# Chunk 1's softmax tiles turned by DMA, half of a key load held behind them, and a new order list

## The chip, the cores and the metric

The kernel runs on one core of one Trainium2 chip. The metric is the device time of one execution in microseconds; of several executions the median is given. A second figure, the span, runs from the first to the last of the program's own instructions in the one execution that was profiled.

## What is computed

Sorted block attention, and behind it a feed-forward layer with a cosine gate. `sort_net` is made nearly doubly stochastic by five rounds of normalising; it mixes the eight key blocks and the eight value blocks of each head; each query block attends to its mixed block alone; the result goes through two matrices.

```python
P = sort_net                                     # (4, 8, 8, 8)
for _ in range(5):
    P = exp(P - max(P, -1)); P = P / (sum(P, -1) + 1e-9); P = P / (sum(P, -2) + 1e-9)
k_sorted = einsum('bhij,bhjcd->bhicd', P, k_b)   # blocks of 96 rows, 8 blocks, d = 64
v_sorted = einsum('bhij,bhjcd->bhicd', P, v_b)
scores = (q_b @ k_sorted^T) / 8                  # 96 x 96 for each block
attn = exp(scores - max); attn = attn / sum
x = (attn @ v_sorted), heads side by side        # (3072, 512)
h = x @ w_in                                     # 512 -> 2048
out = (h * cos(h)) @ w_out                       # 2048 -> 512
```

## The kernel before

The 3072 output rows are cut into eight chunks of 384 rows. Chunk n belongs to batch n // 2 and holds four query blocks u = 0..3 of that batch. Batches 0 and 1 are the first pair, 2 and 3 the second; a pair's keys and values are loaded and sorted together.

The program is one hand-written list, `PLAN`, of some 800 short lines. Each line calls one small function with its numbers, and the order of the lines is the order in which every engine gets its instructions. Nothing reorders them: each engine runs its own in order and waits where a semaphore says so. So the list decides which instruction stands behind which wait. The lines that matter here, for chunk n and block u:

- `S n u` is the score unit: eight matmuls with 128 rows, query block against sorted keys. `T n u` makes the same scores with eight matmuls of 64 rows; two neighbours of these take different halves of the array.
- `M` (VectorE, maximum of the scores), `X` (VectorE, subtract it), `E` (ScalarE, exp, into one of three tiles `p_buf`).
- The softmax tile must be turned before it meets the values. There are two ways. `TP` turns it with eight TensorE transposes into PSUM (tile `pps`) and `TE` copies it to `pT`. `TD` does both with one DMA transpose that SyncE issues.
- `AV` is the product of the turned tile and the sorted values, eight matmuls (tile `av`); `N` divides (VectorE); `XP` and `XE`, or `XD` by DMA, turn the result into `xT`.
- `U n f` (tile `h`, eight matmuls of 384 columns), `C` (ScalarE, the cosine), `G` (VectorE, the product) and `D n t q` (tile `o`, four matmuls of 512 columns: rows t, quarter q of the sum) are the two matrices. `U n f 1` and `U n f 2` run one or both of their halves as twice as many matmuls of 192 columns. `O` copies a finished 128-row block out of PSUM and `W` sends it to DRAM through SyncE.
- `ks`/`kse` sort the keys of batch 1, `vb`/`vbe` its values, `kg`/`kge` the keys of the second pair. `QP`/`QE` turn queries on TensorE.
- `Lpk z 2` loads half z of the second pair's keys into the tile `pair` (128 partitions, 768 KB written); `Lq` loads queries and `Lpv` values. These are issued by GpSimd. `vp2` has GpSimd reorder values from `kv` to `vperm` in four copies. `hp n u` is a tiny GpSimd copy of one column of `pT`: it makes GpSimd, and every load behind it, wait until that tile has been written.

PSUM has three two-bank tiles (`big`) and two one-bank tiles (`acc`). Warm-up matmuls (`keep_warm`) run while the first loads arrive; `MORE` says how many extra pieces they are cut into.

Of the kernel before, what the change touches and what calls it, by code (L numbers as in the profile page):

```python
# [13 lines left out]
ALU = mybir.AluOpType  # L14
AX = mybir.AxisListType

MORE = 55
PLAN = """\
vp 32
kp 0 B 1  # L20
# [116 lines left out]
QE 1 0 1 A  # L137
Lq 2
Lpk 0 2
Lpk 1 2  # L140
G4 1 0
D 0 0 1
vp2 64 128
S 1 2 B
S 1 0 B
M 1 2
S 1 3 B
D 0 1 0
M 1 0
D 0 1 1  # L150
X 1 2
D 0 1 2
X 1 0
E 1 2 1
ks 4 B
D 0 1 3
M 1 3
E 1 0 2
TP 1 2 B
D 0 0 2  # L160
# [60 lines left out]
Lq 3
hk
Lpv 0 6
Lpv 1 6
QE 2 1 0 V
Lpv 2 6
QD 3
zeros 4
C 1 0
G 1 0  # L230
vbe 1 A
vb 0 c
# [46 lines left out]
D 1 0 1
E 2 0 2  # L280
G 1 7
E 2 1 0
S 2 2 B
TD 2 0
D 1 0 2
kg 0 c
kge 0 A
M 2 2
X 2 2
E 2 2 1  # L290
TD 2 1
TD 2 2
S 2 3 B
M 2 3
D 1 0 3
O 1 0 o A
W 1 0
hp 2 2
Lpv 3 6
# [24 lines left out]
AV 2 1
N 2 1
TP 2 3 c
TE 2 3 A
D 1 2 0
AV 2 2
N 2 2  # L330
E 3 0 0
AV 2 3
XP 2 1 B
XE 2 1 V
N 2 3
W 1 1
XP 2 0 c
XE 2 0 V
D 1 2 1
D 1 2 2  # L340
kg 5 B
XP 2 3 B
XP 2 2 c
kge 5 A
XE 2 2 V
XE 2 3 V
D 1 2 3
O 1 2 o V
TD 3 0
W 1 2  # L350
U 2 0
C 2 0
G 2 0
kg 6 B
QD 4
# [36 lines left out]
U 2 6
S 3 2 c 1
M 3 2 1
U 2 7
C 2 6
G 2 6
C 2 7
G 2 7
T 3 3 B  # L400
E 3 1 1
TD 3 1
X 3 2 1
E 3 2 2
TD 3 2
M 3 3
X 3 3
D 2 0 0
D 2 0 1
E 3 3 0  # L410
vgT 0 8 B
TD 3 3
ones 1
AV 3 0
N 3 0
XD 3 0
D 2 0 2
D 2 0 3
O 2 0 o V
W 2 0  # L420
vge 0 8 A
D 2 1 0
vgT 2 8 B
T 4 0 B
AV 3 1
vge 2 8 A
hp 3 3
Lq 5
M 4 0
X 4 0  # L430
D 2 2 0
N 3 1
XD 3 1
D 2 1 1
D 2 1 2
D 2 1 3
O 2 1 o A
AV 3 2
N 3 2
# [64 lines left out]
C 3 6
G 3 6
vge 14 4 A
S 4 2 c 1
M 4 2 1
X 4 2 1
U 3 7  # L510
C 3 7
T 4 3 B
T 5 0 B
G 3 7
M 4 3
X 4 3
E 4 1 2
TD 4 1
E 4 2 0
TD 4 2  # L520
D 3 0 0
D 3 0 1
D 3 0 2
M 5 0
X 5 0
E 4 3 1
TD 4 3
AV 4 0
N 4 0
XD 4 0  # L530
D 3 0 3
D 3 1 0
O 3 0 v A
D 3 1 1
AV 4 1
N 4 1
S 5 1 B
M 5 1
X 5 1
E 5 1 0  # L540
E 5 0 2
XD 4 1
TD 5 0
TD 5 1
QD 6
D 3 1 2
D 3 1 3
AV 4 2
N 4 2
D 3 2 0  # L550
AV 4 3
N 4 3
O 3 1 v A
D 3 2 1
D 3 2 2
# [24 lines left out]
W 3 2  # L580
U 4 3
C 4 3
G 4 3
U 4 5
C 4 5
G 4 5
X 5 2 1
U 4 4
C 4 4
G 4 4  # L590
U 4 6
U 4 7
C 4 6
G 4 6
C 4 7
S 5 3 B
M 5 3
G 4 7
E 5 2 1
TD 5 2  # L600
D 4 0 0
AV 5 0
X 5 3
E 5 3 2
N 5 0
TD 5 3
XD 5 0
D 4 0 1
D 4 0 2
S 6 0 B  # L610
AV 5 1
D 4 1 0
# [15 lines left out]
O 4 0 v A
N 5 2
XD 5 2  # L630
O 4 1 v A
# [12 lines left out]
C 5 1
S 6 3 c 0
D 4 2 3
G 5 1
O 4 2 v V
U 5 0
C 5 0  # L650
G 5 0
U 5 2
C 5 2
U 5 3
QD 7
M 6 3 0
G 5 2
S 6 3 c 1
U 5 4
C 5 3  # L660
G 5 3
X 6 3 0
W 4 0
W 4 1
C 5 4
G 5 4
W 4 2
# [164 lines left out]
def kernel(  # L832
# [16 lines left out]
    B, H, S, D = q.shape  # L849
# [129 lines left out]
    vv = kv[:, :128 * D].rearrange("p (c d) -> p d c", d=D)  # L979
    VQ = 16  # L980

    def v_permute(rows, lo=0, halves=True):

        for z in range(lo, D, VQ):
            dst = vperm[rows, :CD].rearrange("p (d c) -> p d c", d=D)[:, z:z + VQ]
            src = vv[rows, z:z + VQ, :blk]
            if halves:
                dst = dst.rearrange("p d (x t) -> p d x t", x=2)  # L990
                src = src.rearrange("p d (t x) -> p d x t", x=2)
            nc.gpsimd.tensor_copy(dst, src)  # L992
# [72 lines left out]
    V, A = nc.vector, nc.scalar  # L1065
# [31 lines left out]
    E, Q = E_eps[:, :, :nb], Q_eps[:, :nb]  # L1097
# [502 lines left out]
    def spv():  # L1600
# [7 lines left out]
        vp=vp, vp2=vp2, z_vperm=z_vperm, p_pads=p_pads, pk2=pk2, bl2=bl2, sp2=sp2, spv=spv,  # L1608
# [50 lines left out]
```

## Time and profile before

| | us |
|---|---|
| median of 3 runs | 236.79 (236.63 to 240.08) |
| the profiled execution's own time | 237.13 |
| its span | 235.3 |
| TensorE matmuls busy | 226.5 (96% of the span) |
| VectorE busy | 172.3 (73%) |
| ScalarE busy | 151.3 (64%) |
| GpSimd busy | 93.8 (40%) |
| mean granted TensorE clock | 0.998 |

1.8 us of the profiled execution's time lie outside its span. A figure of the chain is time between two events on the path that ended last; the same group has a larger busy time, since a matmul's busy time also holds the time that its result takes to come out, which overlaps the next one.

### The profile page before, as it was taken

How to read it: one execution, taken by the hardware profiler on the slowest of the kernel's cores; microseconds unless marked ns; L12 is line 12 of the kernel's file. 1: busy time of each engine (PE TensorE's matmuls, PEld its weight loads, DVE VectorE, ACT ScalarE, POOL GpSimd, SP SyncE). 2: the span in 40 equal slices, each digit the busy share in tenths (PEclk: the TensorE clock that was granted, in tenths of full speed). 3: DMA queues.
4: the chain of work that ended last, by engine and by line, in shares of the span. 5: the costliest groups of instructions: out<-in, count | busy, mean ns of one | idle time of the engine just before them, and what ended most of it. 6: DMA issues, size and time to landing. Idle time of an engine off the chain costs nothing.

```text
span 235.3 us, 5542 instructions
## 1 busy us (share of the span) xinstructions
PE 226.5 (96%) x2270; PEld 146.0 (62%) x2293; DVE 172.3 (73%) x287; ACT 151.3 (64%) x201; POOL 93.8 (40%) x117
## 2 busy tenths in 40 slices
PE   8889999999999999999999999999999999999994
PEld 8567799667656666645666556654565556456553
DVE  5657986787798786896678976899588868555510
ACT  3365976578969858884888746756567456636531
POOL 7669998795980094981709000720000000000000
PEclk9999999999999999999999999999999999999999
DMA  5999999796799779997999539995942570341012
GB/s 75 225 192 205 205 210 231 121 219 174 110 105 178 152 137 147 135 204 160 148 162 84 80 75 133 219 73 103 168 161 51 100 170 0 63 131 45 0 47 89
DMA packets 67257, 31.11 MB, mean 132 GB/s; under 512 B 55968, under 2 KB 62752, under 8 KB 66976
## 3 DMA queue, kind: packets, MB, share of 16 engines
q0 software_dynamic: 24048, 13.64, 44.0%
q1 hardware_dynamic: 42896, 16.92, 35.2%
q8 instruction: 18, 0.29, 0.5%
q10 hardware_dynamic: 288, 0.20, 0.3%
q14 instruction: 7, 0.06, 0.1%
HBM read 27.27 MB, written 6.29 MB: 143 GB/s over the span
## 4 chain that ended last, share of the span: by engine, by line
PE 82%; DMA 7%; ACT 3%; POOL 3%; DVE 2%; issue 2%; POOLq 0%
PE o L1532 32%; PE h L1487 29%; DMA kv<-in_v_dram 5%; PE h L1510 5%; PE av L1423 3%; PE sc L1319 3%; POOL vperm L992 2%; PE ks L1200 2%; PE xps L1457 2%; PE o L1623 2%; PE pps L1405 1%; DMA kv<-p_buf 1%; PE vs L1256 1%; PE vs L1291 1%; ACT c L1493 1%
## 5 line engine op out<-in xcount | busy, mean ns | idle before, releaser
L1532 PE MATMUL o<-w_out_t,gg 128*128 128x512 bf16 x348 | 84.7, 379 | 1.2 <-issue 0.2
L1487 PE MATMUL h<-xT,w_in_t 128*128 128x384 bf16 x448 | 78.2, 326 | 0.4 <-DVE gg L1499 0.2
L1499 DVE TENSOR_TENSOR gg<-c,h 128x768 bf16<-128x768 f32 x56 | 53.0, 949 | 22.4 <-ACT c L1493 22.3
L1493 ACT ACTIVATE c<-h,half_pi 128x768 f32<-128x768 f32 x56 | 50.5, 901 | 25.5 <-PE h L1487 23.3
L1487 PEld LDWEIGHTS <-w_in_t 128*128 128x128 bf16 x448 | 42.4, 98 | 27.5 <-issue 0.9
L1532 PEld LDWEIGHTS <-gg 128*128 128x128 bf16 x368 | 33.3, 98 | 33.0
L1360 DVE TENSOR_REDUCE mx<-sc 96x8 f32<-96x768 f32 (+1 forms) x41 | 31.5, 771 | 3.1 <-PE sc L1319 1.5
L1378 ACT ACTIVATE p_buf<-s 96x768 bf16<-96x768 f32 x32 | 26.3, 841 | 10.1 <-DVE s L1374 7.7
L992 POOL COPY vperm<-kv 64x1536 bf16<-64x1536 bf16 (+1 forms) x10 | 28.1, 2860 | 2.1 <-DMA kv<-in_v_dram 2.1
L1374 DVE TENSOR_TENSOR s<-sc,mx 96x384 f32<-96x384 f32 (+1 forms) x33 | 24.2, 734 | 1.6
L1435 DVE TENSOR_TENSOR xn<-av,r 96x512 bf16<-96x512 f32 x32 | 22.0, 687 | 1.1
L942 POOL DMA_DIRECT2D kv<-in_q_dram x24 | 16.0, 687 | 0.8 <-issue 0.5
L1069 ACT CAST kTs<-ks 128x512 bf16<-128x512 f32 (+1 forms) x18 | 11.0, 633 | 4.8 <-PE ks L1200 4.8
L942 POOL DMA_DIRECT2D q_mem<-in_q_dram x16 | 10.7, 695 | 3.4 <-DMA kv<-in_v_dram 3.1
L1058 PE MATMUL idle<-warm 128*128 128x128 bf16 (+2 forms) x83 | 9.5, 288 | 2.2 <-ACT q_turned L1141 1.2
L1433 DVE RECIPROCAL r<-av 96x8 f32<-96x8 f32 x32 | 6.3, 198 | 6.6 <-PE av L1423 6.6
L1071 DVE COPY kv<-o 128x512 f32<-128x512 f32 (+1 forms) x6 | 3.7, 624 | 10.0 <-PE o L1623 6.8
L1510 PE MATMUL h<-xT,w_in_t 128*128 128x192 bf16 x128 | 11.1, 246 | 0.0
L1319 PE MATMUL sc<-kTs,q_turned 128*128 128x96 bf16 x160 | 11.1, 206 | 0.0
L1058 PEld LDWEIGHTS <-warm 128*128 128x128 bf16 x101 | 8.9, 121 | 3.4 <-issue 1.3
L1319 PEld LDWEIGHTS <-q_turned 128*128 128x128 bf16 x160 | 9.1, 98 | 2.7 <-DVE s L1374 0.2
L1555 POOL CAST held<-q_turned 96x1 f32<-96x1 bf16 x2 | 0.4, 184 | 26.2 <-DMA q_turned<-q_mem 19.3
(119 smaller groups left out, 272.6 us busy)
## 6 DMA issues: line engine op xcount, KB each, us to landing
out_dram<-kv SPq DMA_DIRECT2D x12, 256.0 KB, 2.9
out_dram<-o_s SPq DMA_DIRECT2D x10, 256.0 KB, 3.0
w_in_t<-in_moe_w_in_dram POOLq DMA_DIRECT2D x4, 512.0 KB, 12.4
w_out_t<-in_moe_w_out_dram POOLq DMA_DIRECT2D x4, 512.0 KB, 11.6
kv<-in_k_dram POOLq DMA_DIRECT2D x2, 768.0 KB, 9.5
kv<-in_v_dram POOLq DMA_DIRECT2D x2, 768.0 KB, 13.3
pair<-in_k_dram POOLq DMA_DIRECT2D x2, 768.0 KB, 10.2
kv<-in_v_dram POOLq DMA_DIRECT2D x6, 256.0 KB, 5.7
```

Source lines behind the costliest of these rows:

```text
L942: nc.gpsimd.dma_start(out=q_heads[:, i, :, e], in_=src[:, ih * IC + i, :, e])
L992: nc.gpsimd.tensor_copy(dst, src)
L1319: nc.tensor.matmul(out, q_of(n, hp)[:, x:x + 128], keys_of(n, u, h2, hp), start=True, stop=True)
L1360: nc.vector.reduce_max(mx[:], s_view(n, u, hp), axis=AX.XY if n < 2 else AX.X)
L1374: nc.vector.tensor_tensor(s, sc, mx.to_broadcast(list(s.shape)), op=ALU.subtract)
L1378: nc.scalar.activation(p[:, :, :blk], s_t.pop((n, u)).rearrange("p e h c -> p (e h) c"), AF.Exp, scale=scale)
L1435: nc.vector.tensor_tensor(xn.rearrange("p h e d -> p e h d"), avv[:, :, :, :D], r.to_broadcast([blk, 2, H2, D]), op=ALU.mult)
L1487: nc.tensor.matmul(o[:, f2, x * w:(x + 1) * w], w_in_t[:, kk, f * 128:(f + 1) * 128], xT[n][:, kk, x * w:(x + 1) * w], start=(kk == 0), st ...
L1493: nc.scalar.activation(c[:], ps["h", n, fp][:, :, :TC], AF.Sin, bias=half_pi[:, 0:1])
L1499: nc.vector.tensor_tensor(gt[n, fp // 2][:, f:f + 2], ps.pop(("c", n, fp))[:], ps.pop(("h", n, fp))[:, :, :TC], op=ALU.mult)
L1510: nc.tensor.matmul(o[:, part, f2 * w:(f2 + 1) * w], w_in_t[:, kk, f * 128:(f + 1) * 128], xT[0][:, kk, h * w:(h + 1) * w], start=(kk == 0) ...
L1532: nc.tensor.matmul(out_ps[n, ts][:], gt[n, q][:, f % 4, ts * 128:(ts + 1) * 128], w_out_t[:, f, :], start=(f == 0), stop=(f == FC - 1))
```

## The change

Three of the four softmax tiles of chunk 1 (u = 2, 0 and 3) are turned by `TD` in place of `TP` and `TE`; u = 1 stays on TensorE. The four GpSimd copies of `vp2 64 128` become four lines `vq`, one copy each. The second half of the second pair's keys, `Lpk 1 2`, is issued behind `hp 1 0`, that is, behind the landing of the turned tile of u = 0. `T 2 2`, `T 2 3`, `T 5 3` and `T 6 0` stand where `S` stood, which makes twelve `T` units. Nine `U` lines get a split, so that twelve groups of four matmuls with 384 columns become eight with 192. `MORE` goes from 55 to 67. And the whole list from chunk 1 on is reordered.

```diff
-MORE = 55
+MORE = 67
...
-Lpk 1 2
 G4 1 0
 D 0 0 1
-vp2 64 128
+vq 64 128 0
 S 1 2 B
 S 1 0 B
+vq 64 128 1
...
-TP 1 2 B
+TD 1 2
...
+TD 1 0
+hp 1 0
+Lpk 1 2
+vq 64 128 2
...
-    def v_permute(rows, lo=0, halves=True):
+    def v_permute(rows, lo=0, halves=True, hi=D):
...
-        for z in range(lo, D, VQ):
+        for z in range(lo, hi, VQ):
...
+    def vq(lo, hi, z):
+        v_permute(slice(lo, hi), z * VQ, True, (z + 1) * VQ)
```

Other moves of the list that the prediction speaks of, in words. On TensorE the product `AV 1 2` stood behind the four quarters of `D 0 1` and the last two of `D 0 0`, with `ks 4` and `TP 1 2` among them, and `S 1 1` came after it; now the same `D` quarters and `ks 4` are ahead of it, `S 1 1` too, and no `TP`. Behind it come three quarters of `D 0 2` and then `AV 1 3`, without the two `TP` that stood between. One of the four copies `QE 2` goes from VectorE to ScalarE, ahead of the first cosine of chunk 1. `kg 0`, which waits for the PSUM tile that `X 2 1 1` frees, stands right behind the first two quarters of `D 1 0`; before, `S 2 2` and the third quarter were ahead of it too. And `D 2 2 0` comes ahead of `AV 3 1` in place of behind it.

VectorE at chunk 1's scores, before (`sc_997` belongs to u = 2, `sc_1006` to u = 0, `sc_1017` to u = 3):

```order
L1360 TENSOR_REDUCE mx_1015<-sc_997 96x8
L1360 TENSOR_REDUCE mx_1031<-sc_1006 96x8
L1370 TENSOR_TENSOR s_1037<-sc_997,mx_1015 96x8x2x48
L1370 TENSOR_TENSOR s_1043<-sc_1006,mx_1031 96x8x2x48
L1360 TENSOR_REDUCE mx_1059<-sc_1017 96x8
L1370 TENSOR_TENSOR s_1078<-sc_1017,mx_1059 96x8x2x48
L1071 CAST kTs_98<-ks_1046 128x2x32x8
```

The same place now (`sc_1005` is u = 2, `sc_1014` u = 0, `sc_1026` u = 3):

```order
L1361 TENSOR_REDUCE mx_1024<-sc_1005 96x8
L1371 TENSOR_TENSOR s_1040<-sc_1005,mx_1024 96x8x2x48
L1361 TENSOR_REDUCE mx_1053<-sc_1014 96x8
L1371 TENSOR_TENSOR s_1055<-sc_1014,mx_1053 96x8x2x48
L1361 TENSOR_REDUCE mx_1057<-sc_1026 96x8
L1371 TENSOR_TENSOR s_1065<-sc_1026,mx_1057 96x8x2x48
L1072 CAST kTs_98<-ks_1067 128x2x32x8
```

The subtraction of u = 2 has moved ahead of the maximum of u = 0, so its exp can start one VectorE instruction sooner.

SyncE from its second instruction to the first query transposes, before:

```order
L1550 DMA out_0_dram<-o_s_1075 128x512
L1550 DMA out_0_dram<-o_s_1106 128x512
L1550 DMA out_0_dram<-c_1201 128x512
L1244 DMA kTs_98<-kTs_98 64x1536
L1245 DMA kTs_98<-kTs_98 64x1536
L962 DMA_TRANSPOSE q_turned1_95<-kv_87 128x16x96 x2
```

The same stretch now; the three `pT` rows are u = 2, u = 0 and u = 3 in this order:

```order
L1397 DMA_TRANSPOSE pT_1043<-p_buf1_107 128x8x96
L1397 DMA_TRANSPOSE pT_1060<-p_buf2_108 128x8x96
L1551 DMA out_0_dram<-o_s_1086 128x512
L1397 DMA_TRANSPOSE pT_1105<-p_buf0_106 128x8x96
L1551 DMA out_0_dram<-o_s_1093 128x512
L1551 DMA out_0_dram<-c_1187 128x512
L1245 DMA kTs_98<-kTs_98 64x1536
L1246 DMA kTs_98<-kTs_98 64x1536
L963 DMA_TRANSPOSE q_turned1_95<-kv_87 128x16x96 x2
```

Two transposes go ahead of the first output block and the third stands behind it.

GpSimd from the query load of chunk 2 on, before (`pair<-in_k_dram` is `Lpk`, the copies to `vperm` are `vp2`):

```order
L932 DMA q_mem_93<-in_q_dram 96x8x256
L905 DMA pair_89<-in_k_dram 128x3072 x2
L992 COPY vperm_88<-kv_87 64x1536 x4
L950 MEMSET kv_87 96x16x64 x2
L942 DMA kv_87<-in_q_dram 96x4x64 x8
```

And now:

```order
L933 DMA q_mem_93<-in_q_dram 96x8x256
L906 DMA pair_89<-in_k_dram 128x3072
L993 COPY vperm_88<-kv_87 64x1536 x2
L1556 CAST held_206<-pT_1060 96x1
L906 DMA pair_89<-in_k_dram 128x3072
L993 COPY vperm_88<-kv_87 64x1536 x2
L951 MEMSET kv_87 96x16x64 x2
L943 DMA kv_87<-in_q_dram 96x4x64 x8
```

The second half of the keys has gone behind two of the four copies and behind the wait for `pT_1060`, the turned tile of u = 0; the last two copies and the zeros and query loads of chunk 3 stand behind that wait too.

More of the change, by code (lines that the diff above doesn't have):

```diff
@@ L224 @@
 Lpv 1 6
-QE 2 1 0 V
 Lpv 2 6
 QD 3
+QE 2 0 0 A
+QP 2 1 c
 zeros 4
+QE 2 0 1 V
+QE 2 1 0 V
+vb 1 B
+QE 2 1 1 V
+vbe 1 V
+U 1 0
 C 1 0
 G 1 0
-vbe 1 A
 vb 0 c
@@ L276 @@
 M 2 1 1
+vb 5 B
+vbe 5 A
+G 1 7
+E 2 0 2
 X 2 1 1
@@ L279 @@
 D 1 0 1
-E 2 0 2
-G 1 7
+kg 0 c
 E 2 1 0
[L283 to L287, printed above, removed]
+T 2 2 B
+T 2 3 B
 M 2 2
 X 2 2
+D 1 0 2
+D 1 0 3
+kge 0 A
+TD 2 0
+TD 2 1
 E 2 2 1
-TD 2 1
+M 2 3
 TD 2 2
-S 2 3 B
-M 2 3
-D 1 0 3
 O 1 0 o A
@@ L319 @@
 X 3 0
+D 1 1 2
 D 1 1 3
+E 2 3 2
 O 1 1 o A
+AV 2 1
 kg 3 B
+D 1 2 0
 kge 3 A
-AV 2 1
+W 1 1
+TP 2 3 c
+kg 5 B
+TE 2 3 A
+AV 2 2
+D 1 2 1
+AV 2 3
 N 2 1
[L326 to L329, printed above, removed]
+XP 2 1 B
 N 2 2
-E 3 0 0
-AV 2 3
-XP 2 1 B
+N 2 3
+XP 2 0 c
+XP 2 2 B
+D 1 2 2
 XE 2 1 V
-N 2 3
-W 1 1
-XP 2 0 c
+XP 2 3 B
+XE 2 2 V
 XE 2 0 V
[L339 to L343, printed above, removed]
 kge 5 A
-XE 2 2 V
 XE 2 3 V
@@ L391 @@
 kswap 1
-U 2 6
 S 3 2 c 1
 M 3 2 1
-U 2 7
+X 3 2 1
 C 2 6
 G 2 6
+U 2 7
 C 2 7
 G 2 7
-T 3 3 B
 E 3 1 1
 TD 3 1
-X 3 2 1
 E 3 2 2
+D 2 0 0
+D 2 0 1
 TD 3 2
+T 3 3 B
+vgT 0 8 B
 M 3 3
 X 3 3
-D 2 0 0
-D 2 0 1
 E 3 3 0
-vgT 0 8 B
-TD 3 3
-ones 1
 AV 3 0
 N 3 0
+TD 3 3
+D 2 0 2
+ones 1
+D 2 0 3
 XD 3 0
-D 2 0 2
-D 2 0 3
 O 2 0 o V
-W 2 0
-vge 0 8 A
 D 2 1 0
@@ L424 @@
 T 4 0 B
+vge 2 8 V
+W 2 0
+hp 3 3
+D 2 2 0
+vge 0 8 A
 AV 3 1
-vge 2 8 A
-hp 3 3
 Lq 5
 M 4 0
+D 2 1 1
 X 4 0
-D 2 2 0
 N 3 1
-XD 3 1
-D 2 1 1
+E 4 0 1
 D 2 1 2
@@ L509 @@
 X 4 2 1
-U 3 7
+U 3 7 2
 C 3 7
+G 3 7
+T 5 0 B
 T 4 3 B
-T 5 0 B
-G 3 7
 M 4 3
 X 4 3
+D 3 0 0
 E 4 1 2
+E 4 2 0
+E 4 3 1
 TD 4 1
-E 4 2 0
 TD 4 2
-D 3 0 0
+D 3 1 0
+D 3 1 1
+AV 4 0
+TD 4 3
+N 4 0
+M 5 0
 D 3 0 1
+XD 4 0
 D 3 0 2
-M 5 0
+D 3 0 3
 X 5 0
[L526 to L532, printed above, removed]
 O 3 0 v A
-D 3 1 1
+S 5 1 B
 AV 4 1
 N 4 1
-S 5 1 B
+E 5 0 2
 M 5 1
@@ L540 @@
 E 5 1 0
-E 5 0 2
 XD 4 1
+D 3 1 2
+D 3 1 3
 TD 5 0
 TD 5 1
-QD 6
-D 3 1 2
-D 3 1 3
+AV 4 3
 AV 4 2
+D 3 2 0
+D 3 2 1
+O 3 1 v A
+D 3 2 2
 N 4 2
[L550 to L555, printed above, removed]
 XP 4 2 B
 XE 4 2 A
+QD 6
 hq 0
 Lq 7
+W 3 0
+N 4 3
 XP 4 3 B
@@ L584 @@
 U 4 5
+W 3 1
+W 3 2
 C 4 5
+M 5 2 1
 G 4 5
-X 5 2 1
 U 4 4
 C 4 4
+U 4 6
 G 4 4
-U 4 6
-U 4 7
 C 4 6
+X 5 2 1
+U 4 7 1
+C 4 7
+T 5 3 B
 G 4 6
-C 4 7
-S 5 3 B
 M 5 3
+E 5 2 1
+D 4 0 0
+TD 5 2
 G 4 7
-E 5 2 1
-TD 5 2
-D 4 0 0
 AV 5 0
 X 5 3
+D 4 0 1
+D 4 0 2
+AV 5 1
+N 5 0
 E 5 3 2
-N 5 0
 TD 5 3
 XD 5 0
[L608 to L612, printed above, removed]
+T 6 0 B
 N 5 1
 XD 5 1
+D 4 1 0
 D 4 0 3
@@ L625 @@
 AV 5 2
+X 6 0
+M 6 1
+X 6 1
+E 6 0 0
+N 5 2
+O 4 0 v A
+XD 5 2
 D 4 1 3
+O 4 1 v A
 AV 5 3
[L628 to L631, printed above, removed]
 D 4 2 0
@@ L653 @@
 C 5 2
-U 5 3
+M 6 3 0
 QD 7
-M 6 3 0
+U 5 3 1
 G 5 2
+U 5 4 1
+X 6 3 0
+C 5 3
 S 6 3 c 1
-U 5 4
-C 5 3
 G 5 3
-X 6 3 0
+C 5 4
 W 4 0
 W 4 1
-C 5 4
+U 5 5
 G 5 4
-W 4 2
-U 5 5
+U 5 6
+M 6 3 1
+X 6 3 1
 C 5 5
 G 5 5
-U 5 6
-C 5 6
 U 5 7
 D 5 1 0
-M 6 3 1
+C 5 6
 G 5 6
-X 6 3 1
 T 7 0 B
@@ L763 @@
 XD 7 0
-D 6 0 0
-D 6 0 1
+AV 7 1
+N 7 1
+XD 7 1
+D 6 1 0
+D 6 1 1
+D 6 1 2
+D 6 1 3
 D 6 0 2
@@ L799 @@
 U 7 2
+W 6 0
+O 6 2 v V
+W 6 1
+W 6 2
 C 7 2
```

283 lines of the change are left out of this document (128 added, 155 removed).

## Prediction

> **What bounds the kernel now.** I read the busy times first, then the stretches, then the chain.
>
> ```profile
> PE 226.5 (96%) x2270; PEld 146.0 (62%) x2293; DVE 172.3 (73%) x287; ACT 151.3 (64%) x201; POOL 93.8 (40%) x117
> PE 82%; DMA 7%; ACT 3%; POOL 3%; DVE 2%; issue 2%; POOLq 0%
> core 0: us, PE busy (x) PEld busy (x) DVE busy (x) ACT busy (x) POOL busy (x), PEclk, DMA share, GB/s
> 44.00:57.00 13.00, 12.89 (x148) 8.14 (x147) 10.93 (x16) 8.35 (x12) 11.94 (x6) 1.00 0.98 193
> 57.00:74.00 17.00, 16.58 (x234) 11.65 (x231) 13.82 (x24) 13.87 (x22) 10.77 (x16) 1.00 0.90 121
> 74.00:100.00 26.00, 25.84 (x247) 16.54 (x249) 21.13 (x35) 20.46 (x30) 14.11 (x15) 1.00 1.12 146
> 100.00:110.00 10.00, 9.57 (x101) 4.84 (x102) 9.02 (x14) 7.18 (x8) 4.96 (x3) 1.00 0.93 181
> 110.00:160.00 50.00, 49.60 (x429) 29.64 (x433) 39.55 (x62) 34.79 (x44) 16.58 (x27) 1.00 0.96 126
> ```
>
> From 44 us on TensorE is never without work for long. In 44 to 57 us, where chunk 1's softmax tiles are turned, it idles 0.11 of 13.00 us; from 57 to 74 us 0.42; from 74 to 160 us 0.16 + 0.43 + 0.40. So a TensorE instruction that goes is worth its whole time, there is little idle time for a new order to win back, and any wait put on TensorE is paid in full. The granted clock (third figure from the end) is full.
>
> **What is removed.** The chain gives the time that units take on TensorE, one behind the other.
>
> ```profile
> 48.98 0.36 PE pps L1405 x8
> 49.34 1.73 PE o L1532 x8
> 51.06 0.26 PE av L1423 x8
> 51.32 0.34 PE sc L1319 x8
> 51.66 0.72 PE pps L1405 x16
> ```
>
> Three units `TP` are the 0.36 at 48.98 and the 0.72 at 51.66: **-1.08 us**, all of it on the path. The copies `TE` go from ScalarE, which was busy 8.35 of 13 us there; I count nothing for them.
>
> **What is added: a wait for a DMA.** `AV 1 2` began at 51.06 us. Now one `TP` less (0.36) and one score unit more (0.34) stand ahead of it, so TensorE reaches it at 51.04. Its turned tile comes from these steps:
>
> ```profile
> 44.65 1.82 DVE L1360 TENSOR_REDUCE mx<-sc 96x8 f32<-96x768 f32 x2 [0.76 <-PE sc L1319]
> 46.39 1.81 DVE L1370 TENSOR_TENSOR s<-sc,mx 96x768 f32<-96x768 f32 x2
> 47.37 1.71 ACT L1378 ACTIVATE p_buf<-s 96x768 bf16<-96x768 f32 x2 [2.21 <-DVE s L1370]
> L1396 SPq DMA_TRANSPOSE pT<-p_buf x2: 1222/1230/1239, 133.1 to 134.4; - x2
> DMA to landing us min/median/max: 2.8/2.8/3.1
> ```
>
> One maximum and one subtraction (1.82 / 2 + 1.81 / 2 = 1.82) from 44.65 end at 46.47; an exp (0.86) ends at 47.35; the transpose is issued at about 47.45. Three such transposes around 133 us, with no load in flight, land in 2.8 to 3.1 us, one 1.3 us after the other. So it would land at 50.3, 0.7 us early. But around 47 us the queues are not empty:
>
> ```profile
> L905 POOL DMA_DIRECT2D pair<-in_k_dram x2: 556/560/564, 43.6 to 44.1; - x2
> ...
> DMA to landing us min/median/max: 8.1/10.2/12.2
> L1550 SPq DMA_DIRECT2D out_dram<-o_s x2: 332/350/369, 49.7 to 51.8; - x2
> ...
> DMA to landing us min/median/max: 5.4/6.2/6.9
> q0 software_dynamic: 125, 0.67, 106.6%
> out_dram<-c SPq DMA_DIRECT2D x1, 256.0 KB, 2.0
> ```
>
> The first half of the keys lands at 43.6 + 8.1 = 51.7 us, the second at 44.1 + 12.2 = 56.3. The two output blocks that SyncE issues at 49.7 and 51.8 take 6.9 and 5.4 us (to 56.6 and 57.2), where the next one takes 2.0. The `q0` row is the whole answer of the queue view for 49.8 to 52.9 us: 0.67 MB, all of it GpSimd's queue. SyncE's, `q1`, moved not one packet in 3.1 us, though its block had been issued before. The same was seen with transposes:
>
> ```profile
> L962 SPq DMA_TRANSPOSE q_turned<-kv x2: 1615/3310/5006, 67.8 to 69.7; - x2
> ...
> DMA to landing us min/median/max: 7.5/7.9/8.4
> q0 software_dynamic: 218, 0.39, 107.8%
> DMA to landing us min/median/max: 2.8/3.0/8.4
> ```
>
> Two query transposes wait from 67.8 us; from 69.5 to 72.0 us only `q0` moves (0.39 MB, value loads), and they land at 75.3 and 78.0. Of all `p_buf` transposes (last row) the slowest, 8.4 us, is the one issued at 85.6 us during value loads. In all three cases SyncE's transfer moves when what GpSimd had queued before it is through.
>
> The change moves the second half of the keys away but leaves the first half where it is. So the transpose of u = 2 gets the engines at about 51.7 us and needs some 1.0 us of its own (they follow each other by 1.3 at most): it lands at 52.7, and TensorE waits 52.7 - 51.04 = **+1.65 us**. The bounds are 0 (it lands at 50.3) and 2.5 (it lands 1.8 after the half). I take the value by the rows of the loads, since they are of the same place. Behind `AV 1 2` in TensorE's order stand three quarters of `D 0 2` and then `AV 1 3`; all of them wait with it, and nothing fills the wait.
>
> Next in SyncE's queue are u = 0 (+1.3, 54.0), an output block and u = 3 (together some 2.2, 56.2). TensorE reaches `AV 1 3` at 52.7 + 0.26 + twelve matmuls of `o` (1.73 x 12 / 8 = 2.60) = 55.56. I take **+0.4 us**, between 0 and 0.7. What GpSimd has behind its new wait moves too:
>
> ```profile
> 44.86 11.25 POOL L992 COPY vperm<-kv 64x1536 bf16<-64x1536 bf16 x4 [0.17 <-DMA kv<-in_v_dram]
> 59.17 1.83 POOL L950 MEMSET kv<- 96x1024 bf16 x2 [3.05 <-issue]
> 81.71 0.50 PE L1319 MATMUL sc<-kTs,q_turned 128*128 128x96 bf16 x8
> ```
>
> It waits for u = 0 until 54.0 and issues the second half by 54.6 (0.56 each), to land some 8 us later, at 62.7. The last two copies (11.25 / 2 = 5.6) end at 60.2. The first value unit that needs them, `vb 4`, stands behind five units `U` of 1.30, `kg 0` behind eight, and these start after 60 (24 matmuls `h` take 3.90, a row further down): in time. The zeros and queries of chunk 3 start at 60.2 in place of 59.17, and their transposes, which landed at 78.0 (69.7 + 8.4, the row above), land some 1 us later; `S 3 0`, which needs them, came at 81.71. No price for these.
>
> **From 57 to 77 us.** The new list keeps the work and changes who waits. TensorE's idle 0.42 us can go, since VectorE and ScalarE get time while TensorE is late. Against it:
>
> ```profile
> 59.92 1.28 ACT L1493 ACT_TABLE_LOAD   x1
> 61.45 0.90 ACT L1493 ACTIVATE c<-h,half_pi 128x768 f32<-128x768 f32 x1 [0.25 <-PE h L1487]
> 74.93 0.55 DVE L1374 TENSOR_TENSOR s<-sc,mx 96x384 f32<-96x384 f32 x1
> 75.40 0.94 DVE L1499 TENSOR_TENSOR gg<-c,h 128x768 bf16<-128x768 f32 x1
> ```
>
> A query copy now stands ahead of the table load at 59.92, on which the first cosine hangs, and with it the first product `G`. And `kg 0` needs the subtraction at 74.93, which now stands behind the 0.94 product in place of ahead of it, while one score unit and one quarter less (0.34 + 0.86) stand before `kg 0` on TensorE. That is a wait of 0 to 0.9. I take **0** for the stretch, with ends -0.4 and +0.9.
>
> **After 77 us.**
>
> ```profile
> 104.41 3.07 DMA kv<-p_buf
> 107.52 0.43 PE av L1423 x8
> 157.71 0.45 PE sc L1346 x16
> 30.60 2.68 PE h L1510 x32
> 166.82 3.90 PE h L1487 x24
> ```
>
> `AV 3 1` waits for its DMA until 104.41 + 3.07 = 107.48; 0.43 of the ten microseconds around it are idle. A quarter `D` (0.86) now goes ahead of it: -0.4. Two neighbouring `T` units take 0.45, two `S` units 0.68: the new pair gives -0.23. The two single ones are bounded by half of that each, -0.23, and by 0; no row here times one by itself between other units, and I take 0. The splits: 96 matmuls of 192 columns at 2.68 / 32 = 84 ns replace 48 of 384 at 3.90 / 24 = 162.5 ns: 8.04 - 7.80 = +0.24. The extra warm-up pieces lie before 15 us, where TensorE waits for other engines; nothing. Together **-0.4 us**, with ends -0.8 and +0.6 for waits of the new order that I didn't follow.
>
> **Sum.** -1.08 + 1.65 + 0.4 + 0 - 0.4 = +0.57 us. Against the profiled execution's own 237.13 (span 235.3) that is 237.7; the median of the runs shown is 0.34 lower, so in its terms 236.79 + 0.57 = 237.36. I give **237.3**. Two per cent, about what a measurement of this kernel can tell from no change, is 4.7 us.
>
> **Rivals.**
>
> *The transposes come in time* (chance 0.28). For it: alone they land in 2.8, with 0.7 to spare, and half of the load that held the outputs back is gone. Against it: the three cases above. Then both waits vanish: -1.08 - 0.4 = -1.5, and 0 to +0.9 from the stretch behind: 235.3 to 236.2, and 234.9 with the -0.4 end of that stretch.
>
> *The second half of the keys overtakes u = 3* (0.10), the slower side. It is issued as u = 0 lands, 54.6 by the sum, when u = 3 stands behind an output block in SyncE's queue. If its packets reach the engines before those of u = 3, that tile lands with the keys, and a half took 56.3 - 51.7 = 4.6 us: u = 3 lands at 56.2 + 4.6 = 60.8, and all that stands behind `AV 1 3` on TensorE comes as much later: 237.3 + 4.6 = 241.9 at most. It decides where u = 3's first packet comes later than about 55.5. The Trainium skill, "DMA: Bandwidth & Descriptors", section on queues, rings and completion order, says that a DMA engine takes turns between queues packet by packet, and that such a packet holds several descriptors; by that u = 3 would share with the second half and not stay ahead of it. The row of 49.8 to 52.9, in which only one queue moved, doesn't look like taking turns. The skill's "TensorE: Matmul & The Clock Gate", part 1, adds that an idle time of about 3.4 us halves the clock for a while; no row here shows it, as TensorE has no such gap.
>
> *The new order costs later* (0.14): VectorE is busy 0.8 of the time up to 160 us, so the order of its work can put further waits of 1 to 1.5 on TensorE: 238.5 to 239.
>
> **Chances.** The forecast, 236.6 to 238.2, has 0.48. From 234.9 to 239.0 reach the forecast, the first rival and the third, 0.90 in all; some 0.1 of it I leave for outer ends of the three: 8 in 10. Faster by over 2% (under 232.05) would need 4.7 us, and the removed units (1.08) and all idle time from 44 to 160 us (1.5) are 2.6: 0.01. Slower by over 2% (over 241.53) is the upper part of the second rival: 0.04.
>
> **What the new profile would show.** Three `TD` of chunk 1 issued near 47.5, 49.4 and 51.4 us that land in over 4 us, the first near 52.7; a wait of TensorE for `pT<-p_buf` of 1 to 2 us ahead of `AV 1 2`, the largest after 21 us; 24 matmuls of `pps` less; the second half of the keys issued near 54.5. If the first lands by 51.0 the first rival holds. I am wrong in kind if the waits are small and the time is still not below 236.

## The result, and the profile after

| | before | changed |
|---|---|---|
| median of 22 runs | 236.71 us | 238.19 us |
| ratio to the kernel before | | 1.0075, 95% interval 1.0057 to 1.0094 |
| the profiled execution's own time | 237.13 | 238.83 |
| its span | 235.3 | 237.1 |

The change made the kernel slower: by 0.75% in the ratio, and by 1.5 us (0.63%) in the medians, since the changed kernel's runs reach further up (237.56 to 242.01 us, against 236.27 to 240.08). 237.3 was predicted. In four of its 22 runs, which took 240.3 to 242.0 us, the mean granted clock was 0.986 to 0.993, in the others 0.998 to 1.00; the ratio leaves out the slowest two of the four. The busy times of the changed kernel's page, in the form of the first row of the prediction (engine, us, share, instructions):

```profile
PE 226.6 (96%) x2329; PEld 147.4 (62%) x2329; DVE 173.9 (73%) x290; ACT 147.5 (62%) x195; POOL 93.9 (40%) x118
```

TensorE is busy as long as before (226.6 against 226.5 us), so what the span gained is time in which it waits. The same stretches as before, from the view of windows (TensorE's busy time is the first number behind the length, the granted clock stands third from the end):

```profile
44.00:57.00 13.00, 11.33 (x110) 6.42 (x109) 10.10 (x15) 5.71 (x8) 9.09 (x7) 1.00 1.01 186
57.00:74.00 17.00, 16.68 (x236) 11.55 (x234) 14.27 (x25) 13.89 (x22) 14.28 (x18) 1.00 1.00 141
74.00:100.00 26.00, 25.55 (x252) 16.02 (x250) 20.55 (x34) 20.30 (x31) 11.80 (x14) 1.00 0.97 145
100.00:110.00 10.00, 9.47 (x103) 5.13 (x102) 9.54 (x15) 7.64 (x9) 7.24 (x4) 1.00 1.05 194
110.00:160.00 50.00, 49.84 (x465) 31.50 (x465) 39.98 (x62) 33.91 (x42) 16.51 (x27) 1.00 0.94 126
```

TensorE's idle time from 44 to 160 us is now 1.67 + 0.32 + 0.45 + 0.53 + 0.16 = 3.13 us, where it was 1.52. The view of TensorE's waits from 44 us to the end names the three that are new (who waits, for what, us in all, times, the longest); the kernel before comes first, then the changed one:

```profile
PE av L1423 <- DMA kv<-p_buf: 0.3, 1, 0.3
PE h L1487 <- DVE gg L1499: 0.2, 1, 0.2
PE o L1532 <- issue: 0.2, 1, 0.2
```

```profile
PE av L1424 <- DMA pT<-p_buf: 1.8, 2, 1.7
PE sc L1347 <- DMA kTs<-kTs: 0.5, 1, 0.5
PE ks L1201 <- DVE s L1375: 0.5, 1, 0.5
```

The first is `AV 1 2` waiting for its turned tile; the second is a `T` unit at 108.9 us and the third `kg 0` at 77.3. How the three transposes of chunk 1 fared stands in the view of the tile `pT` for 47 to 53 us, and two answers of the queue view, for 48 to 51 and for 51.5 to 54 us, show why (queue, packets, MB, share of the 16 engines):

```profile
L1397 SPq DMA_TRANSPOSE pT<-p_buf x3: 1255/1296/1884, 48.1 to 52.5; - x3
DMA to landing us min/median/max: 3.6/3.9/5.1
```

```profile
q0 software_dynamic: 111, 0.65, 105.3%
```

```profile
q1 hardware_dynamic: 1674, 0.64, 116.2%
q0 software_dynamic: 6, 0.00, 0.3%
```

The transpose of u = 2 was issued at 48.1 and landed 5.1 us later, at 53.2. From 48 to 51 us the engines moved GpSimd's first half of the keys and nothing else; from 51.5 to 54 us they moved SyncE's transfers almost alone. TensorE's timeline shows the price:

```profile
51.06 0.50 PE L1320 MATMUL sc<-kTs,q_turned 128*128 128x96 bf16 x8
53.24 0.43 PE L1424 MATMUL av<-vS,pT 96*128 96x65 bf16 x8 [1.67 <-DMA pT<-p_buf]
```

Seven intervals of 42 ns and one matmul separate 51.06 from the place where the product could have begun, near 51.40; it began at 53.24: 1.83 us late, of which 1.67 are idle. The rest is the end of the score matmuls' busy time, in which their results come out; the product would otherwise have overlapped it.

### The profile page after: what moved, and what is told of

Its sections match the earlier page's. It is cut to its first block, busy times and chain, and to the rows that moved or that the text cites. A ratio compares the mean times of both kernels' runs of the same rounds, so it can differ in the third digit from the quotient of the medians.

```text
span 237.1 us, 5643 instructions
## 1 busy us (share of the span) xinstructions
PE 226.6 (96%) x2329; PEld 147.4 (62%) x2329; DVE 173.9 (73%) x290; ACT 147.5 (62%) x195; POOL 93.9 (40%) x118
## 4 chain that ended last, share of the span: by engine, by line
PE 66%; DMA 17%; POOL 8%; DVE 4%; ACT 2%; issue 1%; SPq 0%; POOLq 0%; ACTq 0%
PE o L1533 27%; PE h L1488 27%; DMA kv<-in_v_dram 11%; POOL vperm L993 4%; DMA pT<-p_buf 3%; PE av L1424 3%; DMA kTs<-kTs 2%; DVE gg L1500 2%; PE o L1627 1%; PE ks L1201 1%; POOL w_out_t L978 1%; PE sc L1320 1%; PE sc L1347 1%; PE vs L1292 1%; ACT c L1494 1%; PE xps L1458 1%
## 5 line engine op out<-in xcount | busy, mean ns | idle before, releaser
L1533 PE MATMUL o<-w_out_t,gg 128*128 128x512 bf16 x368 | 87.1, 379 | 0.0
L1488 PE MATMUL h<-xT,w_in_t 128*128 128x384 bf16 (+1 forms) x496 | 78.1, 311 | 0.0
L1500 DVE TENSOR_TENSOR gg<-c,h 128x768 bf16<-128x768 f32 x56 | 52.5, 947 | 20.2 <-ACT c L1494 20.1
L1488 PEld LDWEIGHTS <-w_in_t 128*128 128x128 bf16 x496 | 45.9, 98 | 24.3 <-issue 0.2
L1379 ACT ACTIVATE p_buf<-s 96x768 bf16<-96x768 f32 x32 | 26.2, 840 | 16.8 <-DVE s L1375 12.0
L1070 ACT COPY kv<-o 128x512 f32<-128x512 f32 (+2 forms) x10 | 5.2, 525 | 12.7 <-PE o L1533 9.3
L1511 PEld LDWEIGHTS <-w_in_t 128*128 128x128 bf16 x128 | 10.4, 98 | 0.0
L1070 ACT CAST vS<-vs 96x512 bf16<-96x512 f32 x13 | 7.4, 581 | 4.6 <-PE vs L1257 3.4
L1059 PE MATMUL idle<-warm 128*128 128x128 bf16 (+2 forms) x96 | 8.8, 257 | 1.3 <-DVE half_pi L1042 1.0
```

The costliest lines, as they stand in the source:

```text
L1070: eng.copy(dst, src)
L1379: nc.scalar.activation(p[:, :, :blk], s_t.pop((n, u)).rearrange("p e h c -> p (e h) c"), AF.Exp, scale=scale)
L1488: nc.tensor.matmul(o[:, f2, x * w:(x + 1) * w], w_in_t[:, kk, f * 128:(f + 1) * 128], xT[n][:, kk, x * w:(x + 1) * w], start=(kk == 0), st ...
L1500: nc.vector.tensor_tensor(gt[n, fp // 2][:, f:f + 2], ps.pop(("c", n, fp))[:], ps.pop(("h", n, fp))[:, :, :TC], op=ALU.mult)
L1511: nc.tensor.matmul(o[:, part, f2 * w:(f2 + 1) * w], w_in_t[:, kk, f * 128:(f + 1) * 128], xT[0][:, kk, h * w:(h + 1) * w], start=(kk == 0) ...
L1533: nc.tensor.matmul(out_ps[n, ts][:], gt[n, q][:, f % 4, ts * 128:(ts + 1) * 128], w_out_t[:, f, :], start=(f == 0), stop=(f == FC - 1))
```

## The experiments

Ratios are to runs of the kernel before that were made beside each group, with the 95% interval; the changed kernel itself has 1.0075. Lines of the list are quoted as the program has them.

### 1. Is it the load ahead of the transposes?

Three kernels move the load alone, with the waits that it hangs on; TensorE, VectorE and ScalarE keep their order.

```diff
 both_held:               no_hold:                 staged:
-Lpk 0 2                  +Lpk 1 2 (behind Lpk 0 2) -Lpk 0 2
 ...                       ...                       ...
 hp 1 0                   -hp 1 0                    hp 1 0
+Lpk 0 2                  -Lpk 1 2                  +Lpk 0 2
 Lpk 1 2                                            -Lpk 1 2
                                                     ...
                                                     hk
                                                    +Lpk 1 2
```

In the third, `hk` and the new line stand behind `zeros 3` and ahead of `Lq 3`.

> The changed kernel with the first half of the second pair's keys also issued behind the landing of u = 0's turned tile, so that no load of GpSimd stands ahead of chunk 1's transposes. Queue theory (a SyncE transfer moves only when what GpSimd queued before it is through): the transpose of u = 2, issued at about 48.1 us, lands in some 3 us, near 51, and the 1.7 us wait ahead of AV 1 2 goes; AV 1 3 then comes near 54.4 us, ahead of its tile (issued 51.8, landing near 54.8), and waits about 0.5: 1.2 less than the changed kernel, about 237.0. Own-time theory (a transpose at this place takes 5 us of its own, loads or no loads): the wait stays 1.7 and the time 238.2. Sharing theory (both queues progress together and slow each other): the landing time shrinks only as far as the load overlapped it; here that gives the same 3 us as the queue theory, so this run tells those two from own time only.

Measured: 241.78 us, 1.0207 (1.0190 to 1.0224): far over all that was expected. But the transposes did what the queue theory says (view of `pT`, 46 to 54 us; then TensorE's waits):

```profile
DMA to landing us min/median/max: 2.8/3.0/3.1
```

```profile
PE sc L1320 <- DMA kTs<-kTs: 3.9, 1, 3.9
PE av L1424 <- DMA pT<-p_buf: 0.6, 1, 0.6
```

With no load ahead they land in 3 us and the wait ahead of `AV 1 2` is gone; the 0.6 is `AV 1 3`, as expected. The keys are merely later: they, and the query loads behind them, now meet SyncE's key copies, issued at 59.4 and 60.0 us, which took 7.5 and 8.3 us to land (4.0 before). `S 2 0` waits 3.9 us for them. And behind that wait the windows of 64 to 72 us show the clock:

```profile
64.00:68.00 4.00, 0.48 (x3) 0.09 (x1) 0.58 (x1) 1.51 (x3) 2.32 (x4) 1.00 1.60 171
68.00:70.00 2.00, 1.64 (x11) 1.00 (x12) 2.00 (x4) 0.66 (x1) 1.41 (x4) 0.80 0.67 42
70.00:72.00 2.00, 2.00 (x10) 1.08 (x9) 1.27 (x3) 0.90 (x1) 2.00 (x3) 0.50 0.97 112
```

Behind 3.9 idle microseconds the granted clock falls to 0.50. The chain of this kernel has the next two units `U` at 1.94 and 2.19 us, where they take 1.30 at full clock: 1.5 us more, on top of the 3.9.

> The changed kernel with the second half of the keys issued right behind the first again and without the wait for u = 0's tile. Queue theory: the transpose of u = 2 waits for both halves (drained near 55.8 us instead of 51.2), lands near 57.7, and TensorE waits about 6.2 us ahead of AV 1 2, 4.5 more than in the changed kernel: about 242.7. Sharing theory: by packets in turn the transpose gets half of the engines from 48 us on and lands by 53 to 54: at most 0.8 more, 239.0. Own-time theory: no change, 238.2.

Measured: 244.09 us, 1.0307 (1.0289 to 1.0324). The views of TensorE's waits, of the tile `pT` (46 to 54 us), of the queues for 51.5 to 54.5 us, and three of its windows:

```profile
PE av L1423 <- DMA pT<-p_buf: 6.5, 2, 6.2
```

```profile
DMA to landing us min/median/max: 5.1/8.5/9.7
```

```profile
q0 software_dynamic: 98, 0.58, 95.6%
q1 hardware_dynamic: 91, 0.02, 5.8%
```

```profile
50.00:54.00 4.00, 0.80 (x11) 0.45 (x8) 3.06 (x5) 0.95 (x2) 4.00 (x3) 0.91 1.02 203
54.00:58.00 4.00, 0.96 (x10) 0.69 (x11) 0.24 (x2) 0.84 (x1) 1.86 (x1) 0.50 1.17 213
58.00:60.00 2.00, 2.00 (x6) 0.67 (x5) 0.65 (x1) 0.00 (x0) 0.00 (x0) 0.50 0.55 178
```

The wait is 6.2 us, as the queue theory has it, and the time is 1.4 above its 242.7: again the clock is at 0.50 when TensorE goes on, and in the chain ten `o` matmuls from 57.7 us on take 3.42 us in place of 2.16. So own time is out: one and the same transpose lands in 3.0, 5.1 or 9.7 us by what stands ahead of it. The queue rows correct the theory in one point. For three microseconds, beside the second half of the keys, the queues did not run one after the other; they moved 98 and 91 packets, about one each in turn. GpSimd's key packets have 6,144 bytes (0.58 MB in 98), SyncE's transposes 256 (0.02 MB in 91), so a turn each gives the transpose 4% of the bytes. At 30 packets in a microsecond it is as good as standing behind the load. Beside the first half there was no such sharing: from 48 to 51 us of the same run, with the first transpose issued at 47.3, GpSimd's queue moved 117 packets and SyncE's none. Why the two halves differ isn't shown.

The Trainium skill, "DMA: Bandwidth & Descriptors", section on queues, rings and completion order, says that an engine takes turns between its queues packet by packet; the three microseconds beside the second half agree, with 98 against 91; 117 against none beside the first half, and 111 against none in the changed kernel, do not, so the prediction's doubt was right for those. That a packet gathers some 9 to 17 descriptors, as it says there, does not show: the rows hold 6,144 bytes on one side and 256 on the other. The Trainium skill's "TensorE: Matmul & The Clock Gate", part 1, has the clock halved after some 3.4 us without work: the idle time of 3.9 us agrees, and 1.67 in the changed kernel's profile left it at 1.00. In `no_hold` the clock fell sooner: TensorE stopped at 50.8 us, and a mean of 0.91 over 50 to 54 us means 0.72 us at 0.50, so it fell near 53.3, after 2.5 us.

> The changed kernel with the first half of the keys behind the landing of u = 0's tile and the second half behind the key copies of chunk 2's stage (those that stood behind the keys when both halves were held, which cost 3.9 us and then 8 to 10 matmuls at half clock). Queue theory: the three turned tiles land in 3 us as they did with both halves held; the key copies, issued near 59.4 us, find the first half drained near 60.5 and land near 62.5, ahead of S 2 0 at 64.2; the second half lands near 69, kg 0 takes it at 75. No wait ahead of AV 1 2, 0.6 to 0.7 us ahead of AV 1 3, no clock loss: 238.2 - 1.83 + 0.7 = 237.1. If the key copies wait all the same, 239 or more.

Measured: 243.58 us, 1.0285 (1.0263 to 1.0307). TensorE's waits, and how SyncE's query transposes fared at 72 to 80 us:

```profile
PE av L1424 <- DMA pT<-p_buf: 5.0, 3, 4.1
```

```profile
DMA to landing us min/median/max: 6.8/8.0/9.2
```

The key copies were in time here, as expected, and the wait went one stage further. The second half (64.5 to 71.1 us) pushed chunk 3's queries and the values behind it; the query transposes of SyncE, issued at 73.5 and 77.1, landed late beside the values (from 73.5 to 77 us only GpSimd's queue moved), and the transpose of chunk 2's first tile, behind them in SyncE's queue, was issued only at 81.8 (78.3 in the changed kernel). `AV 2 0` waits 4.1 us for it, and the clock is halved once more. The expectation had looked at the next wait and not at the one behind it.

### 2. Is the wait ahead of AV 1 2 the loss?

```diff
 u2_back:                    av_spread:
-TD 1 2                     -AV 1 2
 ...                          ...
 D 0 1 3                      D 0 2 2, X 1 1, E 1 1 1
+TP 1 2 B                   +AV 1 2
+TE 1 2 A                   +D 0 2 3
                            +TP 1 1 c
                             AV 1 3
                             ...
                            -TP 1 1 c
                             ...
                            -D 0 2 3
```

In the second, `W 0 0` (SyncE) moves with them, ahead of `D 0 2 3`.

> The changed kernel with u = 2 of chunk 1 alone turned on TensorE again (TP and TE), all else kept, the hold behind u = 0 too. Queue theory: the wait of 1.83 us goes, 0.36 us of transposes come back: about 1.4 less than the changed kernel, 236.8. If the time lost lies elsewhere in the new list, the 0.36 only adds: 238.5.

> The changed kernel with TensorE's order alone changed: AV 1 2 goes behind three quarters of D 0 2, the last quarter and TP 1 1 follow, then AV 1 3. Nothing else moves. If the wait ahead of AV 1 2 costs its whole 1.83 us, it is filled here, and what is left is some 0.5 us ahead of AV 1 3, whose tile lands near 56.1 us whatever TensorE does: about 236.9. If something behind (VectorE's chain, the key products) sets the pace anyway, the time stays near 238.2.

Measured: `u2_back` 238.45, 1.0065 (1.0048 to 1.0083); `av_spread` 238.42, 1.0078 (1.0058 to 1.0097). Neither is told apart from the changed kernel. The waits of `u2_back`, then those of `av_spread`:

```profile
PE av L1425 <- DMA pT<-p_buf: 1.2, 2, 0.9
PE h L1489 <- DVE o_s L1073: 0.7, 1, 0.7
```

```profile
PE av L1424 <- ACT pT L1070: 1.0, 1, 1.0
PE av L1424 <- DMA pT<-p_buf: 0.9, 2, 0.7
```

The 1.67 us went, and others came. In `u2_back` TensorE reaches `AV 1 3` earlier and waits 0.9 for u = 3's tile, which was issued at 52.0 and landed in 2.9 us with nothing in its way; later 0.7 more for a copy of VectorE. In `av_spread` the quarter that was drawn ahead had given `TE 1 1` the time to finish, and `AV 1 1` now waits 1.0 us for it. It also shows a fall of the clock that no single idle time explains (its windows):

```profile
54.00:56.00 2.00, 1.30 (x21) 0.90 (x19) 0.72 (x2) 0.20 (x1) 1.96 (x2) 1.00 1.16 229
56.00:58.00 2.00, 0.99 (x31) 0.89 (x27) 1.69 (x4) 1.64 (x3) 2.00 (x2) 1.00 0.76 141
58.00:60.00 2.00, 2.00 (x40) 2.00 (x37) 1.25 (x3) 1.47 (x4) 2.00 (x1) 0.54 0.99 197
60.00:62.00 2.00, 2.00 (x50) 1.85 (x48) 1.05 (x2) 1.07 (x3) 1.09 (x3) 0.61 0.43 143
```

### 3. What does the rest of the new list cost?

```diff
 tp_all: TD 1 2, TD 1 0, TD 1 3 become TP and TE     kg_early:
 u0_only: TD 1 2 and TD 1 3 alone do                +X 2 1 1
 AV 1 2                                               G 1 7
+TP 1 3 c                                             E 2 0 2
 ...                                                -X 2 1 1
+TE 1 3 A
 plain_units:
-U 3 4 2  (and eight more splits)   -T 5 3 B  -T 6 0 B
+U 3 4                              +S 5 3 B  +S 6 0 B
```

> The changed kernel with all three tiles of chunk 1 (u = 2, 0, 3) turned on TensorE again, in the places of the kernel before; the new list is kept otherwise, the second half of the keys still waits for u = 0's tile. Theory: the two waits for turned tiles (1.83 us, and what takes its place) go, 3 x 0.36 us of transposes come back, and what is left above the kernel before is the new list's own cost by the trace: kg 0's wait (0.6), the splits (0.3), the wait of a T unit for key copies at 108 us instead of the one at 107 us (0.2): 236.7 + 0.7 to 1.1 = 237.4 to 237.8. Rival: the new list costs nothing by itself, and all of the loss is the DMA turns: 236.7 or less.

> The changed kernel with u = 2 and u = 3 turned on TensorE again and u = 0 alone by DMA. u = 0's product comes near 55 us, 2 us after its tile landed, so its turn costs TensorE no wait and saves 0.36 us. Theory: 0.36 less than with all three back, 237.0 to 237.4. Rival: a DMA turn costs something whichever tile it is, by the order of SyncE's queue or of GpSimd's loads behind it: as with u = 2 alone back, 238.4.

Measured: `tp_all` 238.30, 1.0070 (1.0053 to 1.0088), slower than expected; `u0_only` 237.97, 1.0051 (1.0036 to 1.0066), 0.6 above its range. The waits of `tp_all`, with a new one at the top:

```profile
PE pps L1409 <- ACT p_buf L1382: 0.6, 1, 0.6
PE ks L1204 <- DVE s L1378: 0.5, 1, 0.5
PE sc L1350 <- DMA kTs<-kTs: 0.4, 1, 0.4
```

The transposes came back, and `TP 1 3`, right behind `AV 1 2`, waits 0.6 for its exp (it starts 0.8 later than it could behind the product). In the kernel before a score unit stood between the two. So these two runs are no clean undoing of the DMA turns: the list has no good place for the unit that it lost. The 0.33 us between their medians is about the 0.36 of the one unit that `u0_only` saves, but their intervals overlap.

> The changed kernel with one VectorE instruction moved: the subtraction X 2 1 1, which frees the PSUM tile of kg 0, ahead of the product G 1 7 as in the kernel before. If that wait of 0.45 to 0.6 us ahead of kg 0 is paid in full, 237.7; if the wait only moves to the next unit, 238.2.

Measured: 238.22, 1.0051 (1.0032 to 1.0069). Its waits:

```profile
PE av L1424 <- DMA pT<-p_buf: 2.2, 2, 2.0
PE sc L1347 <- DMA kTs<-kTs: 0.5, 1, 0.5
```

The row of `kg 0` has gone, so that wait came from `X 2 1 1` behind `G 1 7`. Whether the time fell stays open: the ratio is lower, but the two intervals overlap, and the median is the changed kernel's.

> The changed kernel with the nine added splits of U undone and the two single T units (5 3 and 6 0) made S again; the pair T 2 2, T 2 3 stays. By the changed kernel's trace 48 matmuls of 384 columns (162.5 ns) come back for 96 of 192 (84.5 ns): -0.31 us; a single T unit takes eight matmuls of 24 ns and some 0.2 us around them for the change of shape, 0.40 against 0.34: -0.12 for two. Together 0.4 less, 237.8. If the split units fill waits that the list has without them, the same time or more, 238.2 to 238.6.

Measured: 238.99, 1.0102 (1.0052 to 1.0152): an interval too wide to tell. The profile says that `h` matmuls took 0.22 us less, a little under the 0.31 expected, and that a new wait of 0.25 us ahead of a `U` came up; the size of the split's cost is seen, its worth in the whole is not.

### 4. Putting the pieces right, and one part alone

```diff
 best: u0_only with                 before_u0 (the list before):   hold_only (control):
 D 0 2 0                            -Lpk 1 2                       -Lpk 1 2
+TP 1 3 c                           -vp2 64 128                    -vp2 64 128
+TE 1 3 A                           +vq 64 128 0, 1                +vq 64 128 0, 1
 and kg_early, plain_units           ...                            ...
                                     E 1 0 2                        TE 1 0 A
                                    +TD 1 0                        +hp 1 0
                                    +hp 1 0                        +Lpk 1 2
                                    +Lpk 1 2                       +vq 64 128 2, 3
                                    +vq 64 128 2, 3
                                     ...
                                    -TP 1 0 B
                                    -TE 1 0 A
```

> The pieces together: u = 2 and u = 3 of chunk 1 turned on TensorE, with TP 1 3 behind the first quarter of D 0 2, where its exp has been done (it waited 0.65 us right behind AV 1 2); u = 0 alone by DMA; X 2 1 1 ahead of G 1 7; the splits and single T units undone. From the version with u = 0 alone by DMA (237.97): -0.65 to -0.8 for TP 1 3, -0.4 for kg 0, -0.4 for the units: 236.4, at or a little below the kernel before (236.8). If waits only move on along the list, as they did in the runs so far, 237.3 or more.

> The kernel before, its own list, with one part of the change alone: u = 0 of chunk 1 is turned by DMA, the second half of the keys is issued behind its landing, with the last two of the four GpSimd copies behind that. The transpose, issued near 49.3 us, lands near 53 by the queue theory (behind the first half, drained near 51.2); AV 1 0 comes near 55.2: no wait, and 0.36 us of transposes gone: 236.3. Rival: the second half, 10 us later, pushes the key copies (issued near 60 in the kernel before) and the query transposes behind them, and the time comes back as a wait between 60 and 82 us: 237 to 238.

> The control for the version in which the kernel before has u = 0's DMA turn alone: the second half of the keys is issued behind u = 0's turned tile and ahead of the last two GpSimd copies, as there, but u = 0 is still turned on TensorE. If the 0.6 us that the version gained (0.9969 of the kernel before) come from the eight transposes that left TensorE (0.36), this control stays at the kernel before, 236.7 to 236.9. If moving the load is what pays (less in the queues when the output blocks and key copies are issued), it comes to 236.3 to 236.5 by itself.

Measured: `best` 236.74, 0.9984 (0.9966 to 1.0003); `before_u0` **236.30, 0.9969 (0.9952 to 0.9987)**; `hold_only` 236.95, 1.0016 (1.0000 to 1.0033). The longest wait of `best` from 44 us on, then those of `before_u0` and how its one transpose landed:

```profile
PE av L1426 <- DMA pT<-p_buf: 0.2, 1, 0.2
```

```profile
PE av L1426 <- DMA kv<-p_buf: 0.3, 1, 0.3
PE h L1490 <- DVE gg L1502: 0.2, 1, 0.2
```

```profile
DMA to landing us min/median/max: 3.3/3.3/3.3
```

`before_u0` beats both kernels, the kernel before by 0.3%, clear of its interval. u = 0's tile lands at 52.5 and its product comes after 55: the 3 us of a DMA turn lie beside other work, the eight transposes are gone, and nothing is put in the place of the wait. The interval holds the expected 0.36 us (0.15%); the medians differ by 0.6, and where more than 0.36 would come from isn't shown. The control without the DMA turn is no faster than the kernel before, so it isn't the moved load that pays. `best` removes the waits that experiments 2 and 3 found and with them the whole loss of the new list; it is not shown to be faster than the kernel before. It undoes several pieces at once, so it doesn't say what each of them cost.

## Why the prediction was right, and where it was not

It gave 237.3 and slower by 0.6 us; measured were 238.19 and 1.5. The direction, the largest wait and its cause came as forecast. That 238.19 lies inside the stated 236.6 to 238.2, by 0.01 us, is luck: what came after 57 us was forecast with the wrong sign.

The start of `AV 1 0` splits the sum, since all that the forecast counts up to 57 us lies ahead of it but nothing of the rest. It began at 55.60 us before and at 56.96 now, 1.36 later. Of these, 0.52 were there at the first `AV 0 u` already (last point below), and 0.84 are the change's: -1.08 + 1.83 + 0.07 = 0.82. The forecast had 0.97 for the same three terms. The spans differ by 1.73 us, so some 0.4 more came behind 57 us, where the forecast had -0.4. By its steps:

- **The transposes that go, -1.08 us.** The work is as counted: 24 `pps` matmuls fewer, each 45 ns behind the last.
- **The wait ahead of AV 1 2, +1.65.** Measured 1.83. The landing was forecast 5.25 us after the issue (52.7 - 47.45) and came 5.1 after it, 0.9 after the first half of the keys (44.1 + 8.2 = 52.3). The kernels with the load moved show that the load is the cause. That SyncE's transfer moves only when GpSimd's queue is "through" holds for the first half of the keys; it is too strong for the second. In the kernel before, too, SyncE's queue moved 106 packets beside GpSimd's 63 from 53 to 55.5 us, while the second half was still on its way. The other two transposes landed in 3.9 and 3.6 us, a little under the 4 that were named.
- **AV 1 3, +0.4.** u = 0 landed at 53.8 and u = 3 at 56.1, as forecast (54.0, 56.2), but TensorE was itself 0.5 us later by then, and 0.07 of the wait was left. `both_held` and `u2_back`, where TensorE comes in time, show the wait: 0.6 and 0.9 us.
- **57 to 77 us, 0 with ends -0.4 and +0.9.** The named wait of `kg 0` came at 77.3 us, 0.45 us idle, 0.6 with the overlap that it lost; the idle time that might have gone for it hardly did (0.42 to 0.32). The value taken was too low, the bounds held.
- **After 77 us, -0.4.** This is the step that failed most. The quarter ahead of `AV 3 1` did take that wait away, 0.3 us by the view of waits above and not the 0.43 of all idle time around it. Then a `T` unit at 108 us waited 0.53 for the key copies of SyncE, which were issued 2.1 us later than before (102.2 for 100.1), as the query loads of GpSimd were (86.5 for 84.6): the prediction had seen that these loads come later and had put no price on it. Of the -0.23 of the `T` pair only some -0.14 came. Its sixteen matmuls stand 21 ns apart (0.34 us), and some 0.2 us more go around it where the shape changes, as around a single unit, which so takes some 0.37 where an `S` takes 0.34. The splits cost about what was said.
- **Where the rest is.** In the profiled execution the first product `AV 0 u` began 0.5 us later than before, ahead of all that was changed but the warm-up pieces. In the twelve kernels made from either list it began at 26.2 to 26.9 us (27.2 here, 26.7 before), so I count that to the execution, not to the change.

The rivals: the transposes in time did not happen. `both_held` had them in time and lost far more elsewhere, but its keys came later too, so what transposes in time are worth by themselves isn't shown. The keys did not overtake u = 3, which was through when their first packets came at 55.5. The third, a new order that costs later, was partly so: 0.45 + 0.53 us of idle time at `kg 0` and the `T` unit, against 0.3 won at `AV 3 1`.

What stays open: how much of the 1.5 us belongs to the DMA turns and how much to the new list. By this one profile some 0.8 us come ahead of `AV 1 0` and 0.4 behind it. Yet either part taken back alone left the time about where it was (`u2_back`, `tp_all`, `kg_early`), because each wait that went was followed by another; only the version with all places mended came back to the kernel before.

## What to carry to other kernels

A transpose that moves from TensorE to the DMA buys a short piece of work (0.36 us) with a latency (3 us with empty queues, 5 to 10 behind a load of large packets): do it for a tile whose use is further away than that, as `before_u0` does. Before a load is moved out of the way, follow every transfer that then stands behind it, for two stages and not for one: both halves together turned up as a wait of 3.9 us, and the second half at 64.5 us as one of 4.1, while the second half alone, 10 us later in the kernel before (`hold_only`), cost nothing that could be told. And where TensorE is busy all the time, taking one wait away shows the next: sum the waits along the whole stretch before pricing any of them.

## What the runs showed of the hardware

- Beside the second half of the keys in `no_hold`, two queues that share the engines moved about as many packets each, whatever their sizes: 98 packets of GpSimd against 91 of SyncE in 3 us, 0.58 against 0.02 MB. It is no rule of all such stretches: beside the first half SyncE's queue moved none in 3 us (117 and 111 packets of GpSimd's in `no_hold` and the changed kernel), though its transposes had been issued, and in `both_held`, with no load in flight, its first packets came 1.3 us after the issue.
- The granted clock fell to 0.50 with idle times of 3.9, 4.1 and 6.2 us, which cost 1.3 to 1.5 us each time beside the wait itself. In the profiled run of `av_spread` it fell to 0.54 at 58 to 60 us where no single idle time was longer than 1.0 us, after four microseconds in which TensorE was busy for 1.30 + 0.99 = 2.29. The Trainium skill's "TensorE: Matmul & The Clock Gate", part 1, speaks of a window of some 3.4 us without work; this run does not fit that reading alone. Nor is a low busy time enough: `kg_early` was busy for 2.02 us of 50 to 54, with 2.0 idle in one piece, and kept 1.00. And it differs between runs of one kernel: three of the six of `av_spread` had a mean clock of 0.993, as the profiled one, and three 1.00. What decides it isn't shown.
